# Fourier mixing and a maxout network on one core: earlier places for four planned steps, and the prologue's exponent matmuls held back by one group

## The chip, the cores and the metric

The kernel runs on one core of one Trainium2 chip. The metric is device microseconds of one execution. TensorE (PE) multiplies; VectorE (DVE), ScalarE (ACT) and GpSimd (POOL) work on tiles; SyncE (SP) only issues transfers, one after the other, and so do ACT and POOL for some of them. `PEld` is TensorE's weight load.

## The reference, cut to what matters

```python
X = np.fft.rfft(x, axis=1)                      # x: 8 x 3072 x 256, float32
Yr = Xr @ w_r - Xi @ w_i + b_r                  # w_r, w_i: 256 x 256
Yi = Xr @ w_i + Xi @ w_r + b_i
Yr, Yi = soft(Yr), soft(Yi)                     # sign(v) * max(|v| - 0.01, 0)
y = np.fft.irfft(Yr + 1j * Yi, n=3072, axis=1)
y = y.reshape(8 * 3072, 256)
h = np.maximum(np.maximum(y @ w1, y @ w2), y @ w3)   # 256 x 768 each
out = h @ w_out                                 # 768 x 256
```

## The kernel before

**The mathematics.** The transform of length 3072 = 96 x 32 is taken in two steps by matmuls. Stage `a` multiplies x (96 rows of 32 x 256) by a 96 x 96 table; its result goes through DRAM (`a_d`). Stage `b` reads it back in 12 groups of rows, k = 0 to 11 for each batch, and multiplies by the blocks of the second step (`mb`); stage `w` multiplies by w_r and w_i; the threshold follows; `finish_w` scales the result `u` to `vb`; stage `q` does the first step back and writes DRAM (`z_d`). `load_z` reads eight pieces of it for each batch, `split_z` splits each, and `inverse` does the last step and gives `y`. The network's three products are folded: h = w3 part + relu(y(w2 - w3) + relu(y(w1 - w2))), with the w3 part multiplied through w_out beforehand (`gh`, `gl`).

**The precision.** A value enters TensorE as two f16 halves: ACT makes the high one, DVE the low one, and a product takes three matmuls (`mm3`, L180 to L182). From batch 3 on x is first folded by its symmetry (`sum_x`), then split (`split_x`, tiles `xhl`), then multiplied (`stage_a`, L621).

**The order of the work.** After a prologue the network runs in 384 slots: 8 batches x 8 pieces x 6 blocks of 128 columns; a batch has `SLOTS` = 48. A slot does `up` for one block (tile `pu`, L1112 and L1120 its activations) and, three blocks late, `down` (tile `pd`). The Fourier work of later batches is laid between them: `events` holds (place, step) pairs, places counted in slots, and `run_until` runs those that are due three times in a slot, at its first third, its second and its end. While batch b-1 is in the network, stages b, w and q of batch b run, and stage a of batch b+1. During the last piece of batch b-1 the first piece of `z` of batch b is read and split, and the first `inverse` of batch b runs.

**The steps around the change.** For group k of a batch, `load_a` reads 256 KB of `a_d` into a buffer `ab` (SP, L681; one of the eight `raw` buffers, which x's second half `x2`, the moved `vb` and the weights use too); `split_a` makes the high half (ACT, L692), the low half (DVE, L695) and moves both within the core by four 64 KB transfers (SP, L700); `stage_b` multiplies (tile `px`, L790). `stage_q` of group 11 writes the last rows of `z_d` (ACT, L943; its transfers L947); `load_z` reads a piece of 384 KB (SP, L1012) into the one buffer `zq`; `split_z` makes the halves `zh` and `zl` (ACT L174, DVE L175) and moves them in eight transfers to `ze` (SP, L1062; four where the piece isn't the first of a batch); `inverse` multiplies (tile `pi`, L1077). In the prologue, groups k = 0 to 11 of batch 0 run in a loop, with the weights' loads (`load`), maxima (`largest`, L373), exponents (`exponent_of`) and splits (`phase`) laid out by `planned(k, ...)`.

`exponent_of` turns a tile's column maxima into one exponent: DVE reduces to a column (`col`, L270), TensorE spreads it (tile `pt`, L274), DVE finishes. All behind the column goes through `later`: in the slots it waits for a later third; in the prologue it is called at once:

```python
    def later(fn):
        if "slot" in st:
            waiting.append((st["slot"], fn))
        else:
            fn()
```

The framework gives each engine's instructions their final order. It takes what it reckons ready, earlier places in the program first; so a place is a rank, not a time. Instructions traced `in_turn` stay behind the slot's last activation, and `load_a` behind the last `load_z`.

Of the kernel before, what the change touches and what calls it, by code (L numbers as in the profile page):

```python
# [101 lines left out]
def fourier_maxout_kernel(  # L102
# [12 lines left out]
    NJP = 12  # L115
    SLOTS = NCH * NF
    NATIVE = 2 * NCH
    HALF_X = 3 * NCH
# [8 lines left out]
    st = {}  # L127
# [6 lines left out]
    def split_scaled(hi, lo, src, scale):  # L134
        h = hi if hi.dtype == F16 else hi.bitcast(F32)
        nc.scalar.activation(out=hi, in_=src, func=AF.Copy, scale=scale)
        return nc.vector.scalar_tensor_tensor(
            out=lo, in0=src, scalar=scale, in1=h, op0=ALU.mult, op1=ALU.subtract
        )
# [5 lines left out]
    def later(fn):  # L145
        if "slot" in st:
            waiting.append((st["slot"], fn))
        else:
            fn()

# [17 lines left out]
    def split_later(hi, lo, src, scale=None):  # L168
        h = hi if hi.dtype == F16 else hi.bitcast(F32)
        if scale is None:  # L170
            nc.scalar.activation(out=hi, in_=src, func=AF.Copy)  # L171
            later(lambda: nc.vector.tensor_tensor(out=lo, in0=src, in1=h, op=ALU.subtract))  # L172
        else:
            nc.scalar.activation(out=hi, in_=src, func=AF.Copy, scale=scale)  # L174
            later(lambda: low(nc.vector.scalar_tensor_tensor(  # L175
                out=lo, in0=src, scalar=scale, in1=h, op0=ALU.mult, op1=ALU.subtract
            )))
# [62 lines left out]
    def load_fft_weights():  # L240
        ws = raw_tile("wst").rearrange("p (k c) -> p k c", k=KD)
        for i, w in enumerate((w_r, w_i)):
            nc.sync.dma_start(
                out=ws[:, :, i * D:i * D + D], in_=w.rearrange("(k p) d -> p k d", p=P)
            )
        return [ws[:, kd] for kd in range(KD)]

    def load_tables():
        rows = [b.rearrange("(r o d) -> r o d", r=1, o=1) for b in (b_r, b_i)]
        for c in range(2):  # L250
            nc.sync.dma_start(out=bias[64 * c:64 * c + 64, 0:1], in_=rows[c].broadcast_to([64, 1, D]))
        nc.sync.dma_start(out=qf, in_=mq[:, 0:2])
        nc.sync.dma_start(out=id_sb, in_=ident)
        st["tiled"] = s_tile("tiled")[:, 0:P]
        nc.sync.dma_start(out=st["tiled"], in_=mq[:, 26])
# [7 lines left out]
    def small(name, dt=F32, bufs=1):  # L263
        return fft.tile([P, 1], dt, name=name, bufs=bufs)
# [33 lines left out]
    def limits(name, total, one):  # L298
        low, add = small("low" + name), small("add" + name)
        nc.vector.tensor_scalar(  # L300
            out=low, in0=total, scalar1=-1.0, scalar2=one + 1.0, op0=ALU.mult, op1=ALU.add
        )
        nc.vector.tensor_scalar(out=low, in0=low, scalar1=28.0, scalar2=254.0, op0=ALU.max, op1=ALU.min)
        nc.vector.tensor_scalar(out=add, in0=total, scalar1=1.0, scalar2=-one, op0=ALU.mult, op1=ALU.add)
        return low, add
# [3 lines left out]
    def scale_fft_weights(ws):  # L309
        mx = fft.tile([P, KD], F32, name="mxc", bufs=1)  # L310
        for kd, t in enumerate(ws):
            nc.vector.tensor_reduce(
                out=mx[:, kd:kd + 1], in_=t[:, 0:2 * D], axis=AX.X, op=ALU.max, apply_absolute_value=True
            )
        def scales(e):
            st["lim", "x"] = limits("x", e, 142.0)
            st["sc"] = power("sc", e, -1.0, 267.0, 1)

        exponent_of(mx, "c", 23, 0xFF, 28.0, scales)
# [34 lines left out]
    class Weights:  # L354
# [83 lines left out]
        for v in range(0, FF, HALF) for i in range(3) for kd in range(KD)  # L438
    ], less=True)
    w_dn = Weights("d", [  # L440
        (woh[:, f], wol[:, f], out_v2[f * P:(f + 1) * P],
         out_v2[f * P:(f + 2) * P].rearrange("(k p) w -> p k w", p=P) if f + 1 < NF else None,
         [t[:, f:f + 2] for t in (woh, wol)] if f + 1 < NF else None)
        for f in range(NF)
    ])
# [32 lines left out]
    def pump(new=True):  # L478
        for u in list(reversed(running)):
            phase(*u)  # L480
            if not made[u]:
                running.remove(u)
        if units and new:
            running.append(units.pop(0))
            phase(*running[-1])
# [5 lines left out]
    def at(pos, fn, i, k=None, n=None):  # L491
        if n is None or 0 <= k < n:
            events.append((pos, len(events), fn, i))
# [482 lines left out]
    for q in range(EARLY, NB * NCH):  # L976
        b, i = divmod(q, NCH)
        p = i if b == 1 else 9 + 5.2 * i if b == 2 else (b - 2) * SLOTS + 5.6 * i
        at(p - (3 if b == 1 else 5 if b == 2 else 8), load_x, q)
        if q >= HALF_X:  # L980
            at(p - 1, sum_x, q)
        at(p, split_x, q)
        at(p + 1, stage_a, q)
        if q >= HALF_X:
            p = 9 + 5 * i if b == 3 else (b - 3) * SLOTS + 5.5 * i + 5
            at(p - 4, load_m, q)
            at(p, largest_m, q)
            if i == NCH - 1:
                at(p + 1, scale_m, b)
    for b in range(1, NB):  # L990
        for k in range(-2, NJP + 1):
            p = 8 + 2.13 * (k + 2) if b == 1 else (b - 1) * SLOTS - (1.2 if b > 2 else 0.4) + 2.72 * (k + 2)
            for d, fn, i in (
                (0, load_a, k + 3), (-1.4, split_a, k + 1), (1.6, finish_w, k - 1), (1, stage_b, k + 1),
                (4, stage_q, k - 1), (2, stage_w, k), (2.4, stage_w2, k),
            ):
                at(p + d, fn, b * NJP + i, i, NJP)
            if k == -2:
                at(p, load_a, b * NJP)

    def run_until(pos):
        while events and events[0][0] <= pos:
# [165 lines left out]
    def load_first_blocks(i, n=6):  # L1168
        k = slice(i, i + n)
        nc.sync.dma_start(out=mb_f[:, k], in_=mq[:, 2 + i:2 + i + n])  # L1170
# [25 lines left out]
    def planned(k, fn, *args):  # L1196
        plan[k].append((fn, args))
# [11 lines left out]
    planned(3, w_dn.load, 0)  # L1209
    planned(4, lambda: w_dn.load(2, [fft.tile([P, 2, D], F32, name="ru", tag="u", bufs=2) for _ in range(2)]))  # L1210
    planned(6, w_dn.load, 4)
    for k, n in ((4, 0), (5, 2), (5, 3), (7, 4)):
        planned(k, w_dn.largest, n)
    planned(7, w_dn.scale)
    for k, n in ((5, 0), (7, 2)):
        planned(k, prepare, w_dn, n)
        planned(k + 3, phase, w_dn, n)

    for k in range(-3, NJP + 1):
        for fn, i in (  # L1220
            (load_a, k + 3), (stage_b, k + 1), (stage_w, k), (finish_w, k), (stage_q, k - 1),
        ):
            if 0 <= i < NJP:
                if fn == stage_q and i == NJP - 1:
                    total = small("total")
                    nc.vector.tensor_tensor(out=total, in0=w_up.e, in1=w_dn.e, op=ALU.add)
                    st["lim", "u"] = limits("u", total, 271.0)
                fn(i)
        with tc.issue_after(st["ld"].ins):
            if k == -3:  # L1230
                fft_weights = load_fft_weights()
                load_first_blocks(2, 4)
            if k == -2:
                load_tables()
            if k == 0:
                scale_fft_weights(fft_weights)
                split_scaled(*(t.rearrange("p a b -> p (a b)") for t in (qh, ql, qf)), Q_SCALE)
            if k == 0:
                split_scaled(ft[:, 0], ft[:, 1], st["tiled"][:, 64:P], F_SCALE)
                split_scaled(qt[:, 0], qt[:, 1], st["tiled"][:, 0:64], Q_SCALE)  # L1240
            if k in (-2, 1, 4):
                load_first_blocks(2 * k + 10)
            for fn, args in plan[k]:
                fn(*args)
            if k == 6:
                whole = ga_sb.rearrange("p i e n m -> p (i e n m)")
                nc.sync.dma_start(out=whole, in_=ga[:, 0:2 * N2 * N1])
                first = fft.tile([N1, NQ * D], F32, name="xm", bufs=1).bitcast(F16)[:, 0:2 * NT]
                nc.sync.dma_start(out=first, in_=ga[:, 2 * N2 * N1:])
                st["ga"] = first.rearrange("p (i n m) -> p i n m", i=2, n=NQ)  # L1250
            if 7 <= k < 12:
                load_x(NCH + k - 7)
            if k == 8:
                units += [(w_up, n) for n in (6, 8, 10)] + [(w_dn, n) for n in (3, 4)]
            if k in (8, 9, 10):
                pump()
# [130 lines left out]
```

## Time and profile before

| | |
|---|---|
| time, median of 3 runs | 1776.3 us (1773.79 to 1778.37) |
| the profiled execution | 1774.88 us, of which the span is 1772.8 us |
| PE busy | 98% of the span, 15747 matmuls |
| DVE, ACT, POOL busy | 68%, 66%, 16% |
| mean granted TensorE clock | 0.997 |
| transfers | `zq<-z_d` 384.0 KB, `ab<-a_d` 256.0 KB, `ab<-ab` 64.0 KB, median 4.5, 4.7 and 3.1 us to landing |

A row of the timeline gives the start, the length, the engine (`SPq` is a transfer being issued), the line, what is written and read, the shape, how many instructions are merged, and in brackets the engine's idle time before it and what ended that.

### The profile page before, as it was taken

The numbers are of one execution on the slowest core, as the hardware profiler recorded it, in microseconds if no ns is written. First come the engines' busy times: TensorE is split into PE (matmuls) and PEld (weight loads), VectorE is DVE, ScalarE is ACT, GpSimd is POOL, SyncE is SP. The second block draws the span as 40 slices with busy tenths as digits, with TensorE's granted clock in tenths as the row PEclk, the third lists the DMA queues.
The fourth block names the chain that finished last, engine by engine and source line by source line (L and its number), as shares of the span: only waits on it lengthen the run. The fifth ranks groups of instructions, "written<-read, shape, count | busy, mean of one in ns | idle before, by whom it ended". The sixth has DMA issues, their size and how long they took to land.

```text
span 1772.8 us, 40996 instructions
## 1 busy us (share of the span) xinstructions
PE 1732.1 (98%) x15747; PEld 1253.5 (71%) x15747; DVE 1211.4 (68%) x2525; ACT 1164.4 (66%) x2445; POOL 277.2 (16%) x505
## 2 busy tenths in 40 slices
PE   9999999999999999999999999999999999999999
PEld 4766777667776777767776677776777777777776
DVE  2887887577865788667875688766786467644332
ACT  4777676676765777666765677666776566655554
POOL 1001012112221112112221112211212100110000
PEclk9999999999999999999999999999999999999999
DMA  9766565467655577457765667555664444422111
GB/s 295 243 173 182 160 174 153 145 177 200 173 147 154 155 190 201 128 153 188 184 165 155 160 166 213 152 141 146 169 168 122 120 109 115 121 76 62 55 56 35
DMA packets 201936, 269.52 MB, mean 152 GB/s; under 512 B 30862, under 2 KB 149998, under 8 KB 201646
## 3 DMA queue, kind: packets, MB, share of 16 engines
q1 hardware_dynamic: 169502, 193.34, 42.3%
q0 software_dynamic: 24608, 66.62, 11.5%
q10 hardware_dynamic: 7632, 6.95, 1.4%
q8 instruction: 124, 2.03, 0.5%
q14 instruction: 70, 0.57, 0.1%
HBM read 124.31 MB, written 75.50 MB: 113 GB/s over the span
## 4 chain that ended last, share of the span: by engine, by line
PE 75%; DMA 8%; DVE 6%; issue 5%; ACT 4%; SPq 2%; POOL 0%; ACTq 0%; DVEq 0%; POOLq 0%
PE pu L180 11%; PE pu L182 11%; PE pu L181 11%; PE pd L180 8%; PE pd L182 8%; PE pd L181 8%; PE py L180 3%; PE py L182 3%; PE py L181 3%; PE pi L1077 3%; DMA ab<-ab 2%; PE px L790 2%; PE pz L958 2%; PE pa L621 2%; ACT zh L174 1%
## 5 line engine op out<-in xcount | busy, mean ns | idle before, releaser
L180 PE MATMUL pu<-yh,wuh 128*128 128x384 f16 x1536 | 501.9, 327 | 0.2 <-ACT pu L1112 0.2
L182 PE MATMUL pu<-yh,wul 128*128 128x384 f16 x1536 | 501.0, 326 | 0.0
L181 PE MATMUL pu<-yl,wuh 128*128 128x384 f16 x1536 | 501.0, 326 | 0.0
L172 DVE TENSOR_TENSOR hh<-h,hh 128x384 f16<-128x384 f32 x384 | 212.7, 554 | 187.3 <-ACT hh L171 186.9
L180 PE MATMUL pd<-woh,hh 128*128 128x256 f16 x1152 | 314.1, 273 | 1.1 <-ACT o L1157 1.0
L182 PE MATMUL pd<-woh,hh 128*128 128x256 f16 x1152 | 314.1, 273 | 0.0
L181 PE MATMUL pd<-wol,hh 128*128 128x256 f16 x1152 | 313.9, 273 | 0.0
L1112 ACT ACTIVATE pu<-pu 128x384 f32<-128x384 f32 x384 | 184.2, 480 | 185.1 <-PE pu L182 174.9
L171 ACT ACTIVATE hh<-h 128x384 f16<-128x384 f32 x384 | 199.9, 520 | 71.9 <-DVE h L1116 65.2
L182 PEld LDWEIGHTS <-wul 128*128 128x128 f16 x1536 | 150.3, 98 | 99.8 <-issue 0.7
L180 PEld LDWEIGHTS <-wuh 128*128 128x128 f16 x1536 | 150.2, 98 | 92.7 <-issue 21.7
L181 PEld LDWEIGHTS <-wuh 128*128 128x128 f16 x1536 | 150.3, 98 | 72.8 <-issue 1.7
L631 POOL DMA_DIRECT2D a_d<-aq x160 | 94.6, 595 | 608.3 <-ACT aq L628 605.9
L1159 POOL DMA_DIRECT2D out_dram<-o x189 | 104.4, 558 | 461.6 <-ACT o L1157 456.9
L1120 ACT ACTIVATE h<-pu 128x384 f32<-128x384 f32 x258 | 125.4, 486 | 67.5 <-PE pu L182 64.2
L180 PE MATMUL py<-wch,tt 128*128 128x256 f16 x504 | 137.4, 273 | 1.3 <-ACT zs L964 0.6
L180 PEld LDWEIGHTS <-hh 128*128 128x128 f16 x1152 | 112.6, 98 | 35.2 <-issue 10.5
L182 PE MATMUL py<-wch,tt 128*128 128x256 f16 x504 | 137.4, 273 | 0.0
L181 PE MATMUL py<-wcl,tt 128*128 128x256 f16 x504 | 137.3, 272 | 0.0
L175 DVE SCALAR_TENSOR_TENSOR zl<-zq,s0u,zh 96x1024 f16<-96x1024 f32 (+1 forms) x70 | 81.6, 1173 | 80.4 <-ACT zh L174 80.4
L1091 DVE SCALAR_TENSOR_TENSOR y<-pi,ye 128x192 f32<-128x192 f32 x252 | 109.6, 508 | 33.9 <-ACT ye L1085 33.6
L181 PEld LDWEIGHTS <-hh 128*128 128x128 f16 x1152 | 112.7, 98 | 26.4 <-issue 1.9
(261 smaller groups left out, 3116.5 us busy)
## 6 DMA issues: line engine op xcount, KB each, us to landing
zq<-z_d SPq DMA_DIRECT2D x63, 384.0 KB, 4.5
out_dram<-o POOLq DMA_DIRECT2D x189, 128.0 KB, 3.6
ab<-a_d SPq DMA_DIRECT2D x84, 256.0 KB, 4.7
ab<-ab SPq DMA_DIRECT2D x336, 64.0 KB, 3.1
vb<-vb SPq DMA_DIRECT2D x308, 64.0 KB, 3.0
z_d<-zs POOLq DMA_DIRECT2D x70, 256.0 KB, 3.8
xm<-in_x_dram SPq DMA_DIRECT2D x40, 384.0 KB, 4.0
a_d<-aq POOLq DMA_DIRECT2D x160, 96.0 KB, 3.4
```

The lines of the kernel that those rows point to most:

```text
L171: nc.scalar.activation(out=hi, in_=src, func=AF.Copy)
L172: later(lambda: nc.vector.tensor_tensor(out=lo, in0=src, in1=h, op=ALU.subtract))
L175: later(lambda: low(nc.vector.scalar_tensor_tensor(out=lo, in0=src, scalar=scale, in1=h, op0=ALU.mult, op1=ALU.subtract)))
L180: nc.tensor.matmul(o, lh, rh, start=start, stop=False, **kw)
L181: nc.tensor.matmul(o, lh, rl, start=False, stop=False, **kw)
L182: st["mm"] = nc.tensor.matmul(o, ll, rh, start=False, stop=stop, **kw)
L631: nc.gpsimd.dma_start(out=av[1 - r, :, :, n:n + 512], in_=o[64 * h:64 * h + 48])
L1077: st["mm"] = nc.tensor.matmul(pv[:, e, n2], st["z"][e][:, n2, h * P:(h + 1) * P], ga_sb[:, i, e, c * NQ + n2], start=i == 0, stop=i == 1,)
L1091: nc.vector.scalar_tensor_tensor(out=yv[:, e], in0=pv[:, 0], scalar=(1 - 2 * e) * Y_SCALE, in1=ev, op0=ALU.mult, op1=ALU.add,)
L1112: st["act"] = nc.scalar.activation(out=p, in_=p, func=AF.Relu)
L1120: st["act"] = nc.scalar.activation(out=h32, in_=p, func=AF.Relu, scale=H_SCALE)
L1159: q.dma_start(out=out_v[b, c, t], in_=o)
```

## The change

Five edits, in the order of the diff:

1. `later` gets a third way: where `st["held"]` is a list, the step is put on it. The prologue's loop empties the list after each group's five steps and, for k = 0 to 10, starts a new one ahead of that group's planned work. An exponent's matmul and all behind it so come after the next group's stages.
2. `split_x` of batches 3 to 7 stands 0.4 slots earlier.
3. `split_a` stands at -2.2 in place of -1.4 slots (batches 3 to 7), or -1.6 (batches 1 and 2).
4. `stage_q` of group 11 stands at 3 in place of 4 slots; `load_a` of group 0 stands 2.5 slots earlier (batches 3 to 7).
5. In the prologue, the last maximum of w_out and its exponent move from k = 7 to k = 8; the splits of two pieces of w_out come at k = 9 and 10 (before: 8 and 10).

```diff
     def later(fn):
         if "slot" in st:
             waiting.append((st["slot"], fn))
+        elif "held" in st:
+            st["held"].append(fn)
         else:
             fn()
...
-        at(p, split_x, q)
+        at(p - 0.4 * (q >= HALF_X), split_x, q)
...
             for d, fn, i in (
-                (0, load_a, k + 3), (-1.4, split_a, k + 1), (1.6, finish_w, k - 1), (1, stage_b, k + 1),
-                (4, stage_q, k - 1), (2, stage_w, k), (2.4, stage_w2, k),
+                (0, load_a, k + 3), (-2.2 if b > 2 else -1.6, split_a, k + 1), (1.6, finish_w, k - 1),
+                (1, stage_b, k + 1), (4 if k < NJP else 3, stage_q, k - 1), (2, stage_w, k), (2.4, stage_w2, k),
             ):
                 at(p + d, fn, b * NJP + i, i, NJP)
             if k == -2:
-                at(p, load_a, b * NJP)
+                at(p - (2.5 if b > 2 else 0), load_a, b * NJP)
...
-    for k, n in ((4, 0), (5, 2), (5, 3), (7, 4)):
+    for k, n in ((4, 0), (5, 2), (5, 3), (8, 4)):
         planned(k, w_dn.largest, n)
-    planned(7, w_dn.scale)
+    planned(8, w_dn.scale)
     for k, n in ((5, 0), (7, 2)):
         planned(k, prepare, w_dn, n)
-        planned(k + 3, phase, w_dn, n)
+        planned(9 + n // 2, phase, w_dn, n)
...
                 fn(i)
+        for fn in st.pop("held", ()):
+            fn()
+        if 0 <= k < NJP - 1:
+            st["held"] = []
```

Here p = (b - 1) * 48 - 1.2 + 2.72 * (k + 2) for batches 3 to 7, with k from -2 to 12.

## Rows read from the trace of the kernel before

**Rows 1.** The page, part 1: busy time, share, instructions.
```profile
PE 1732.1 (98%) x15747; PEld 1253.5 (71%) x15747; DVE 1211.4 (68%) x2525; ACT 1164.4 (66%) x2445; POOL 277.2 (16%) x505
```
**Rows 2.** Waits of PE: us in total, times, longest.
```profile
PE px L790 <- DMA ab<-ab: 13.3, 10, 3.4
PE pi L1077 <- DMA ze<-zl: 7.1, 10, 1.1
...
PE pa L621 <- DVE xhl L175: 2.2, 7, 0.3
...
PE pd L180 <- ACT o L1157: 1.0, 1, 1.0
```
**Rows 3.** Timeline of PE: two matmuls, one behind the other.
```profile
778.77 0.27 PE L182 MATMUL pd<-woh,hh 128*128 128x256 f16 x1
778.88 0.27 PE L180 MATMUL pd<-woh,hh 128*128 128x256 f16 x1
```
**Rows 4.** Timeline of DVE and PE in the prologue, 76 to 78 us.
```profile
76.37 0.69 DVE L373 TENSOR_REDUCE mwd<-rw 128x2 f32<-128x512 f32 x1 [3.35 <-DMA rw<-in_moe_w_out_dram]
...
77.79 0.49 PE L274 MATMUL pt<-id_sb,col 128*128 128x128 f32 x2 [3.01 <-DVE col L270]
```
**Rows 5.** Timeline of PE: stage b's waits, group 0 of batches 3 to 6, then group 11.
```profile
565.39 0.28 PE L790 MATMUL px<-mb_all,ab 128*128 128x64 f16 x4 [1.27 <-DMA ab<-ab]
566.52 0.51 PE L790 MATMUL px<-mb_all,ab 128*128 128x64 f16 x12 [0.86 <-DMA ab<-ab]
...
778.20 0.51 PE L790 MATMUL px<-mb_all,ab 128*128 128x64 f16 x12 [2.01 <-DMA ab<-ab]
...
991.97 0.51 PE L790 MATMUL px<-mb_all,ab 128*128 128x64 f16 x12 [1.79 <-DMA ab<-ab]
...
1204.47 0.51 PE L790 MATMUL px<-mb_all,ab 128*128 128x64 f16 x12 [3.39 <-DMA ab<-ab]
...
1543.21 0.94 PE L790 MATMUL px<-mb_all,ab 128*128 128x64 f16 x16 [1.13 <-DMA ab<-ab]
```
**Rows 6.** Timeline of ACT and SP ahead of the wait at 778.20.
```profile
765.84 1.14 ACT L174 ACTIVATE zh<-zq,s0u 96x1024 f16<-96x1024 f32 x1
...
769.29 0.62 ACT L692 ACTIVATE ab<-ab 128x512 f16<-128x512 f32 x1
...
771.33 0.58 SPq L1012 DMA_DIRECT2D zq<-z_d  x1
772.01 1.24 SPq L700 DMA_DIRECT2D ab<-ab  x2
```
**Rows 7.** The chain that ended last: start, length.
```profile
772.64 5.43 DMA ab<-ab
```
**Rows 8.** The page, part 6: issuer, count, size, median us to landing.
```profile
zq<-z_d SPq DMA_DIRECT2D x63, 384.0 KB, 4.5
...
ab<-a_d SPq DMA_DIRECT2D x84, 256.0 KB, 4.7
ab<-ab SPq DMA_DIRECT2D x336, 64.0 KB, 3.1
```
**Rows 9.** Stretches: busy time (instructions) of PE, PEld, DVE, ACT, POOL; clock; DMA.
```profile
567.78:571.19 3.41, 3.41 (x30) 2.31 (x28) 1.78 (x5) 0.80 (x3) 0.00 (x0) 0.50 0.92 241
...
779.41:782.82 3.41, 3.41 (x29) 2.26 (x28) 1.68 (x4) 0.85 (x3) 0.00 (x0) 0.50 0.73 241
...
1201.00:1204.40 3.40, 0.08 (x3) 0.00 (x0) 1.16 (x2) 1.18 (x3) 0.27 (x1) 1.00 1.00 265
```
**Rows 10.** Timeline of ACT at the first and the last change of batch.
```profile
321.31 0.47 ACT L1112 ACTIVATE pu<-pu 128x384 f32<-128x384 f32 x1 [0.68 <-PE pu L182]
...
325.06 1.33 ACT L174 ACTIVATE zh<-zq,s0u 96x512 f16<-96x512 f32 x2 [0.63 <-issue]
...
1587.90 0.47 ACT L1112 ACTIVATE pu<-pu 128x384 f32<-128x384 f32 x1 [0.84 <-PE pu L182]
1588.29 1.32 ACT L174 ACTIVATE zh<-zq,s0u 96x512 f16<-96x512 f32 x2
```

## The prediction, on record before the changed kernel ran

> **What bounds the kernel.** I read the page's busy shares first, and in them TensorE alone: it is busy for 98% of the span, the next engine for 68% [rows 1]. So a change pays here only where TensorE stands idle, or where its clock is halved; the same work done sooner on another engine pays nothing by itself. The list of TensorE's waits came second. The reader is to see that few reasons hold nearly all of it: stage b waits for the moved halves of `ab` (13.3 us), the inverse for those of z (7.1 us), stage a for the low half of x (2.2 us) [rows 2], and one exponent's matmul in the prologue for its column (3.0 us) [rows 4]. Third came the timeline of each wait, for what is late ahead of it. One correction holds for all of them: a matmul's record is 0.27 us long while the next one starts 0.11 us behind it [rows 3], so TensorE really loses about 0.16 us more at each wait than the row says.
>
> Fourth I read the granted clock by stretches. Behind the waits of batches 3 and 4 it stands at 0.50, the lower of its two levels (1.2 GHz), for 3.41 us, in each of two places [rows 9]. At half the rate each such stretch costs half its length, 1.7 us. The longest wait left the clock at 1.00 although TensorE was busy for 0.08 of 3.40 us [rows 9], so a wait doesn't always bring this on.
>
> **The change, part by part.** No matmul, activation or byte is added. Everything moves.
>
> *The prologue.* DVE stands for 3.35 us until a load of w_out has landed, reduces it at 76.37, and TensorE, whose queue has the exponent's matmul in the middle of a group's eight, stands for 3.01 us [rows 4]. With the reduction one group later and its matmul behind the following group's stages, TensorE has a whole group's products between them. Gain 3.0 + 0.16 = 3.2 us. The lower bound is nothing: DVE may still meet the load early and hold up a threshold behind it. What follows (the exponents' small steps, the splits of w_out) gets one group's time less and is needed only in the network. I take the upper end, because DVE's wait alone stopped nothing here; TensorE stopped at the matmul.
>
> *The first group of batches 3 to 6.* Five rows: 1.27 + 0.86 + 2.01 + 1.79 + 3.39 = 9.3 us [rows 5], with five tails of 0.16 10.1 us. What is late is seen at 778.20. ACT makes the high half at 769.29; SP issues the read of the next z piece at 771.33 and the second pair of moves only at 772.01 [rows 6]; the last of that pair takes 5.43 us from issue to landing [rows 7], against a median of 3.1 us for this transfer [rows 8]. After the change `split_a` is due one slot earlier (a slot is 4.6 us on average, the span over 384), directly behind the split of z at 765.84, whose 1.14 us end at 766.98 [rows 6]: 2.3 us earlier. At 2.3 us all waits but the last would be gone and that one would keep 1.1 us. But the moves would also be ready ahead of the read of z, which waits for the same `zl`, and the 2.3 us by which they now exceed the median would go too, together 4.6 us. I take the whole 10.1 us; the lower bound is 2.3 us less at the batch with 3.39 us and nothing where the read stays ahead and ACT is crowded, some 5 us. The earlier first `load_a` is what makes the split possible there: it must have landed a slot sooner. The two half-clock stretches stand right behind two of these waits; without them 3.4 us more. Their lower bound is nothing, as I can't tell what else lowers the clock.
>
> *Later groups.* Every split of these batches moves by 0.8 slots. At group 11 of batch 7 the wait is 1.13 us [rows 5], with its tail 1.3 us, and a slot covers it. The other waits of the 13.3 us are 2.9 us in four places (13.3 less 9.3 and 1.1), two of them in batches 1 and 2, where the split moves by only 0.2 slots. I take 1.0 us of them; bounds nothing and 2.9. Sum 2.3 us.
>
> *v's last group.* The last rows of z are written a slot sooner, so z's first piece is read sooner. But its split can't begin ahead of the slot's own activation. At the first change of batch that one starts at 321.31 and the split at 325.06, so 3.3 us can be won; at the last they are at 1587.90 and 1588.29, back to back, and nothing can [rows 10]. Taking at each of the seven changes the smaller of this room and of the wait there gives 4.6 us, of the 7.1; with the tails of the three that vanish 5.2 us. Bounds nothing and 7.1.
>
> *x split sooner.* Seven waits of 0.3 us, 2.2 us together [rows 2]; a third of a slot is over a microsecond and covers each. With tails 3.3 us; I take two thirds, 2.2, because this split now comes next to those of z and `ab` in a batch's first slot, which lengthens ACT's queue there. Bounds nothing and 3.3.
>
> *What the moves cost.* New neighbours make new small waits. Those that the list shows today where nothing was planned, like the 1.0 us of `pd` for `o` [rows 2], are what I go by: four of that length, 4 us. The bounds are nothing and the 8 us of the first rival.
>
> Sum: 3.2 + 10.1 + 3.4 + 2.3 + 5.2 + 2.2 - 4 = 22.4 us. The profiled execution has 1774.9 us, 1.5 below its median (its span 1772.8 and 2.1 around it, in which nothing changes); 22.4 off the median of 1776.3 gives 1754.
>
> **A rule weighed against this.** The pair of moves behind the 384 KB read took 5.43 us, the median is 3.1 [rows 7, 8]: what SP issued ahead was served first. The Trainium skill, "DMA: Bandwidth & Descriptors", section "Queues, rings and completion order", says that SP has one ring on each of the 16 DMA engines and that descriptors are consumed in ring order; the trace agrees, by these 2.3 us. The rule speaks for the moves that now pass the read of z, and against the first `load_a`, which may now stand in front of z's moves.
>
> **The rivals.** *The early read in front of z's moves.* The 256 KB of `load_a` are now due while z's eight moves go out, on which the inverse waits. 384 KB cost 2.3 us, so 256 KB cost 1.6 us; at five changes of batch (for batches 3 to 7) 8 us, in place of the 4 that I subtract: a gain of 18, and if the inverse's 5.2 us go with it 13: a time of 1758 to 1763, say 1761. For it: the inverse has no room today, all its waits end with these moves. Against: in the plan the last rows of `a_d` stand at 40.2 slots and the read at 44.3, so it may be through before z's moves begin. By the rule named above the price is the same, as order in the ring is all it tells.
>
> *The order stays.* A place is only a rank; if the framework keeps the read of z ahead of the second pair and the splits where they are, only the exponent's 3.2 us remain, with small gains: 1772. Against: the split stands one slot later than its neighbour z and follows the slot's activation, which a rank does change.
>
> *The early read blocks SP: slower.* If the framework puts the first `load_a` ahead of z's moves and its buffer or the last rows of `a_d` aren't there, SP stands and z's moves stand behind it; TensorE then waits at `pi`. It decides from 22.4 / 5 = 4.5 us at each of the five changes on; at 6 us the kernel takes 1784. For it: all of these steps share SP. Against: eight `raw` buffers, of which at that place I count at most five held (two `ab`, two `x2`, one `vb`).
>
> **The numbers.** Chances: forecast 0.60, the read in front 0.16, the order stays 0.15, SP blocked 0.09. A difference of 0.3%, 5.3 us, is about what a measurement of this kernel can tell from no change. Faster by more: the first two and a little of the third, 0.77; within: 0.14; slower: 0.09. The range reaches up to 1773, which leaves out the blocked queue and part of the third case, and down to 1745, where the upper ends of all terms would lie (3.2 + 10.1 + 3.4 + 4.4 + 7.1 + 3.3 = 31.5): together under 2 in 10.
>
> **What would show it.** Right: no wait of `pt` near 75 us; no wait of `px` at the first group of batches 3 to 6, ACT's `ab` within a microsecond behind `zh`, the moves of `ab` issued ahead of the read of z; the clock at 1.00 there; the waits of `pi` gone at three changes of batch and kept at the others. Wrong: `pi` waits above 7.1 us with `load_a` issued among z's moves (first rival); `px` waits as before with the read between the pairs (second); SP idle until `a_d` or a buffer (third). The prediction fails most likely at the 4 us for new waits, which no row of the kernel before can show.

## The result and the profile after

The changed kernel takes 1745.8 us (median of 4 runs, 1742.64 to 1747.86), the kernel before, run beside it, 1775.1 (4 runs, 1771.74 to 1778.37). The ratio is 0.983, 95% interval 0.981 to 0.986: 29 us faster. The forecast was 1754 with a range from 1745; the time lies at that range's lower edge. The profiled execution took 1742.64 us, of which 1740.8 are the span: 32.0 less than the span before. In the changed file the lines stand two further down (L790 is L792, L1077 is L1079, L692 is L694).

The page's busy shares, of the kernel after:

```profile
PE 1721.4 (99%) x15747; PEld 1249.0 (72%) x15747; DVE 1208.6 (69%) x2525; ACT 1161.8 (67%) x2445; POOL 277.9 (16%) x505
```

The same 15747 matmuls, and 10.7 us less busy time [rows 1]: part is clock, part is records that had been stretched by waits inside (the X edit, below). TensorE's waits in the kernel after (us in total, times, longest):

```profile
PE pi L1079 <- DMA ze<-zl: 2.6, 4, 0.9
PE px L792 <- DMA ab<-ab: 1.6, 2, 0.9
PE pz L773 <- DVE mxu L755: 1.5, 1, 1.5
...
PE pd L182 <- ACT o L1159: 0.8, 2, 0.4
```

`px` for `ab` falls from 13.3 to 1.6, `pi` from 7.1 to 2.6, `pa` for `xhl` L175 and `pt` for `col` have left the list [rows 2, 4]. One wait is new, 1.5 us of the prologue's `pz`. The timeline at the network's change from batch 2 to 3 and of the opening of batch 4 behind it, where the wait of 2.01 us had been [rows 5, 6] (ACT, then SP, then PE):

```profile
750.79 1.14 ACT L176 ACTIVATE zh<-zq,s0u 96x1024 f16<-96x1024 f32 x1
751.83 0.61 ACT L694 ACTIVATE ab<-ab 128x512 f16<-128x512 f32 x1
...
733.17 0.39 SPq L683 DMA_DIRECT2D ab<-a_d  x1
...
736.82 1.16 SPq L1064 DMA_DIRECT2D ze<-zh  x2
...
753.26 1.14 SPq L1064 DMA_DIRECT2D ze<-zl  x2
754.49 2.67 SPq L702 DMA_DIRECT2D ab<-ab  x4
757.22 0.58 SPq L1014 DMA_DIRECT2D zq<-z_d  x1
...
761.13 0.63 PE L792 MATMUL px<-mb_all,ab 128*128 128x64 f16 x16
```

`split_a` follows the split of z at once, all four moves are issued ahead of the next read of z, and `px` begins without a wait. Counted from z's split (765.84 before, 750.79 after), ACT makes the high half 2.4 us sooner. But SP is still issuing z's moves until 754.40, so the last of the four moves is issued only 1.0 us sooner [rows 6]. The rest is time to landing. The second pair of moves, in the kernel before and then after (from the issues: count, size, median us to landing):

```profile
ab<-ab SPq DMA_DIRECT2D x2, 64.0 KB, 5.4
```
```profile
ab<-ab SPq DMA_DIRECT2D x2, 64.0 KB, 2.1
```

The early 256 KB read goes out 3.65 us ahead of z's first moves, not among them; at the other four changes it is 3.2 to 4.3 us. At four of the five SP had first stood idle in front of it until the last rows of `a_d` had landed. SP's waits from 727 to 735 us (us in total, times, longest):

```profile
SPq L683 <- DMA a_d<-aq: 4.2, 2, 4.0
```

It held nothing up, because z's moves became due only behind the read. Stretches behind the former waits of batches 4 and 6 (busy time of PE, PEld, DVE, ACT, POOL; granted clock; DMA share; GB/s):

```profile
761.00:765.00 4.00, 4.00 (x58) 3.24 (x57) 2.53 (x5) 2.88 (x8) 0.83 (x2) 1.00 0.99 327
1174.00:1178.00 4.00, 4.00 (x59) 3.22 (x57) 2.14 (x4) 3.04 (x8) 1.67 (x3) 1.00 1.00 305
```

The clock stays at 1.00 (2.4 GHz), with the transfer engines at least as full as before [rows 9]. In the whole execution no stretch is at 0.50 but the very end; before there were three of 3.41 us, two behind `px` and one at 31.89 in the prologue.

Where the 32.0 us came from I read by slots: the start of the first `pu` of each of the 384 slots in both traces, and where the difference of the two steps.

| place | gain in the traces, us | term of the forecast, us |
|---|---|---|
| prologue, up to the first `pu` (111.83 to 107.93), its new waits included | 3.9, of it 1.7 the clock at 31.89, 1.1 more ahead of group 3, 1.1 behind it | 3.2 |
| openings of batches 3 to 6, in order 3.4, 3.2, 2.1, 3.8, and 1.2 in the two slots behind | 13.7 | 10.1 + 3.4 |
| later groups (0.6, 0.6, 1.6) | 2.8 | 2.3 |
| x split: 4 x 1.02, 1.82, 0.34 | 6.2, of it 2.2 also with a's edits alone | 2.2 |
| `pi` rows, 7.1 to 2.6 | 4.5 | 5.2 |
| new small waits, all else | about 1 gained | -4 |

### The profile page after: what moved, and what is told of

It is laid out like the page before. It is cut to its first block, busy times and chain, and to the rows that moved or that the text cites. A ratio compares the mean times of both kernels' runs of the same rounds, so it can differ in the third digit from the quotient of the medians.

```text
span 1740.8 us, 40997 instructions
## 1 busy us (share of the span) xinstructions
PE 1721.4 (99%) x15747; PEld 1249.0 (72%) x15747; DVE 1208.6 (69%) x2525; ACT 1161.8 (67%) x2445; POOL 277.9 (16%) x505
## 4 chain that ended last, share of the span: by engine, by line
PE 81%; issue 6%; DVE 4%; DMA 4%; ACT 3%; SPq 1%; POOL 0%; ACTq 0%; DVEq 0%; POOLq 0%
PE pu L182 12%; PE pu L184 12%; PE pu L183 12%; PE pd L182 8%; PE pd L183 8%; PE pd L184 8%; PE py L182 3%; PE py L184 3%; PE py L183 3%; PE pi L1079 3%; PE px L792 2%; PE pa L623 2%; PE pz L960 2%; PE pa L640 1%; DMA z_d<-zs 1%
```

## The experiments

Ratios are to the kernel before run beside each of them, with a 95% interval; gains are that ratio times the time before.

**One part at a time.** The four parts, each alone in the kernel before. The X edit:

```diff
-        at(p, split_x, q)
+        at(p - 0.4 * (q >= HALF_X), split_x, q)
```

> Of the change only x's split 0.4 slots earlier. By the prediction's term (seven waits of 0.3 us with tails of 0.16 us each) at most 3.3 us less, the seven waits of pa for xhl gone. By the rival, that a wait at these matmuls, four of which run side by side in the array, hides more than its record shows: 5 to 6.5 us less, about 1.0 us at the eighth slot of each of four batches, with the same rows gone.

Measured 1769.8 us, 0.999 (0.997 to 1.001): no change. The waits of `pa` are gone, but new waits of `px` have come. Of this run, a line of the list of waits; one of the new ones, from PE's timeline; a wait in the prologue, from PE's timeline; and the stretch around it, with the columns of the stretches above:

```profile
PE px L790 <- DMA ab<-ab: 14.5, 13, 2.8
```
```profile
1229.48 0.51 PE L790 MATMUL px<-mb_all,ab 128*128 128x64 f16 x12 [1.15 <-DMA ab<-ab]
```
```profile
74.40 2.05 PE L771 MATMUL pz<-uf,qf 128*128 128x512 f32 x2 [2.75 <-DVE mxu L760]
```
```profile
73.70:83.90 10.20, 7.03 (x19) 5.19 (x20) 5.06 (x23) 6.04 (x11) 0.00 (x0) 0.50 0.79 198
```

The total of 14.5 us says little, as three runs below whose network is that of before have 10.8 to 14.3. But three of these waits (0.50, 0.23 and 1.15 us) stand in the slot right behind one that the edit shortened, where no other run has one, and those slots are 0.66, 0.38 and 1.31 us longer: there the gained time is handed on to the next wait for a transfer. That it stays where those are gone, the times don't show (1749.8 us without X and 1748.8 with it, below). The stretch at half clock is chance: the prologue is the same as before here, yet it met a second wait. This run also shows what a wait at `pa` hides. The twelve small `pa` matmuls of one group in the kernel before, and then those of this run:

```profile
584.18 0.64 PE L621 MATMUL pa<-xhl,zeros 48*64 48x512 f16 x4
585.14 0.40 PE L621 MATMUL pa<-xhl,zeros 48*64 48x512 f16 x2 [0.32 <-DVE xhl L175]
...
585.81 0.62 PE L621 MATMUL pa<-xhl,zeros 48*64 48x512 f16 x6
586.36 0.28 PE L182 MATMUL py<-wch,tt 128*128 128x256 f16 x1
```
```profile
588.36 1.16 PE L621 MATMUL pa<-xhl,zeros 48*64 48x512 f16 x12
589.44 0.28 PE L180 MATMUL py<-wch,tt 128*128 128x256 f16 x1
```

Without the wait the twelve take 1.08 us to the next product; with it 2.18, of which two `py` in between are 0.2. So 0.9 us are lost where the row says 0.32: these matmuls run beside each other, their records overlap, and idle time counts only from the end of the last. The slot is 0.87 us shorter in this run at four places. The tail here is about 0.55 us, not the 0.16 of full-size matmuls.

The edits of a's split and first read:

```diff
-                (0, load_a, k + 3), (-1.4, split_a, k + 1), (1.6, finish_w, k - 1), (1, stage_b, k + 1),
+                (0, load_a, k + 3), (-2.2 if b > 2 else -1.6, split_a, k + 1), (1.6, finish_w, k - 1), (1, stage_b, k + 1),
...
-                at(p, load_a, b * NJP)
+                at(p - (2.5 if b > 2 else 0), load_a, b * NJP)
```

> Of the change only a's first read 2.5 slots and a's splits 0.8 (0.2) slots earlier. Forecast by the sum's terms: 10.1 + 3.4 + 2.3 = 15.8 us less, px waits gone at group 0 of batches 3 to 6, both half-clock stretches behind them gone. Rival: the read stands in front of z's moves, pi waits grow from 7.1 to about 15 us, and the gain is about 8 us. Second rival: without x's split moved too, ACT's first slots are crowded and half of the px waits stay: 7 us.

Measured 1759.3 us, 0.993 (0.990 to 0.995): 13.1 us. `px` for `ab` is at 1.9 us in 4 places, and the four openings gain 3.39, 3.18, 2.07 and 3.79 us, to 0.01 us as in the whole change, each against the one trace of before. `pi` stays (8.2 us).

The edit of v's last group:

```diff
-                (4, stage_q, k - 1), (2, stage_w, k), (2.4, stage_w2, k),
+                (4 if k < NJP else 3, stage_q, k - 1), (2, stage_w, k), (2.4, stage_w2, k),
```

> Of the change only v's last group multiplied a slot earlier. Forecast by the room between the slot's activation and z's split: 4.6 us of pi waits gone (batches 1, 2 and 4 in the main, 5.2 us with tails), those at the changes to batches 3, 5, 6 and 7 left within 0.4 us. Rival: all waits but those of the last two changes go, because they hang on other things than z's read: over 5.5 us. Third: the waits stay because the moves to ze are held by SP: under 1.5 us.

Measured 1766.0 us, 0.997 (0.995 to 0.999): 5.3 us. `pi` falls to 4.8 us (6.5 to 8.3 in the runs with v's place of before and SP's queue untouched), and no change of batch is without a wait: some 0.4 us is left at five of the seven, 1.0 and 1.7 at the others.

The prologue: `later` with its held list, and w_out's maximum, exponent and splits at k = 8, 9 and 10 (the rest of the diff).

> Of the change only the prologue (the held exponents and w_out's maximum a group later). Forecast: the 3.0 us wait of pt gone, first slot 3.2 us sooner, and nothing else: 3.2 us less. Rival: the new wait of pz for a threshold, 1.5 us near 94 us, belongs to the prologue's change and is paid back: 1.7 us less. If the first slot comes 3.9 us sooner or more, the clock's half stretch near 32 us has gone with it.

Measured 1769.3 us, 0.998 (0.997 to 1.000): 3.2 us. `pt` no longer waits; `pz` waits 1.5 and 0.9 us for `mxu` in its place. The four parts sum to 1.8 + 13.1 + 5.3 + 3.2 = 23.4 us, 2 to 6 less than the whole in its two measurements (25.4 and 29.4). Each of these numbers is uncertain by 3 to 6 us, so that the whole is more than its parts isn't shown.

**The whole, and the whole less one.** The changed kernel again; without the X edit; without the early `load_a`.

> The whole change once more, beside the four part runs: for adding up. First measured ratio 0.9834, so about 29 us less than the kernel before. If the parts of the first four runs (13.1, 5.3, 3.2 and 1.8 us by their ratios) simply add, 23.4 us; if x's part is worth more where a's split has moved too, 27 to 30 us.

> The change without x's earlier split. If the parts add, it is 1.8 us (the part alone) behind the whole change. Theory: alone, x's split was laid ahead of a's split on ACT and DVE in a batch's first slot and so lengthened the px waits (14.5 us there, 13.3 before), which hid what it gave; with a's split moved it gives 5 to 6 us, at slot 8 of four batches about 1.0 us each, so this kernel is 5 to 6 us behind the whole change, with seven or eight pa waits in its list and px waits as short as in the whole change.

> The change without the earlier read of a's first rows (their split still a slot sooner). Theory of the prediction: the read is what lets the split stand there; without it the split waits on ACT for the landing, about 1 us at batches 3 to 6, the px waits stay short since there are 3 us of room, and the time is within 2 us of the whole change. Rival: ACT stands in order behind the late read, the activations of pu with it, and half of the px waits come back: 5 to 8 us behind the whole change. Rival on the queue: the early read costs z's moves 1.6 us at five changes of batch, so without it the kernel is 3 to 8 us faster.

Measured 1748.8 us, 0.986 (0.982 to 0.989), for the whole; 1749.8, 0.987 (0.983 to 0.990), without X; 1750.4, 0.986 (0.983 to 0.990), without the early read. In time the three can't be told apart. The traces can. Without X the four slots lose 0.67 us each and two others 1.0 and 0.3, together 4.0; the rest of the 6.2 in the table stands in the trace of a's edits alone (4 x 0.35 and 0.8). `pi` waits again at three changes where the whole kernel has none (0.35, 0.57, 0.40 us; the slots lose 0.73, 0.52, 0.45). So a part of `pi`'s gain is the X edit's, though why isn't shown. Of these 5.7 us the medians show 1.0: in the same two traces other slots go the other way, the two largest by 1.2 and 1.0 us. Without the early read the four openings gain exactly what they gain with it (3.40, 3.18, 2.07, 3.79), with the split in the same place; about 0.35 us of `pi` comes back at three changes, and a wait of `pa` for ACT's `hh` opens elsewhere (1.6 us, with a stretch at half clock behind it).

**Is it the order in SP's queue, or the full engines?** The kernel before, in which ACT issues the second pair of group 0's moves:

```diff
-                    nc.sync.dma_start(
+                    (nc.scalar if i and k % NJP == 0 else nc.sync).dma_start(
                         out=both[64 * i:64 * i + 64, :, b], in_=parts[64 * b:64 * b + 64, i]
```

> The kernel before, with the two moves of a's low halves of group 0 issued by ACT in place of SP: in batches 3 to 6 nothing else in any engine's order differs, and the split stands as late as before. By the order of the queue (the moves are late because SP's 384 KB read of z stands ahead of them) they land about 2.3 us sooner, the px waits fall from about 11 to 14 us to 3 to 6, and the kernel is 5 to 9 us faster. By the rival, that the DMA engines are simply full there, the moves land as late as before and nothing changes beyond 2 us.

Measured 1767.1 us, 0.996 (0.994 to 0.998): 7.3 us, with the split as late as before. A line of the list of waits; from the timeline the same opening of batch 4 (ACT and SP) and the wait that stayed, of batch 3 (PE); and the pair at the opening of batch 4 among the issues:

```profile
PE px L790 <- DMA ab<-ab: 5.2, 6, 3.2
```
```profile
770.65 0.61 ACT L692 ACTIVATE ab<-ab 128x512 f16<-128x512 f32 x1
772.54 1.29 ACTq L700 DMA_DIRECT2D ab<-ab  x2
...
772.68 0.58 SPq L1012 DMA_DIRECT2D zq<-z_d  x1
...
567.85 0.51 PE L790 MATMUL px<-mb_all,ab 128*128 128x64 f16 x12 [3.19 <-DMA ab<-ab]
```
```profile
ab<-ab ACTq DMA_DIRECT2D x2, 64.0 KB, 4.3
```

The moves still go out beside the 384 KB read, but in another queue. The kernel stands 1.36 us later here than before [rows 6], so they are issued 0.83 us sooner; the wait that vanished was 2.01 us, and at batch 6 3.39 us became 0.23. From issue to landing they now take 4.3 us at batches 4 and 5, against 5.4 and 5.3 behind the read in SP's queue, and they still land 0.4 us behind the read. Ahead of the read, in the kernel after, it is 2.1. So of the 3.3 us between first and last in the queue, 1.0 to 1.1 are the order in SP's queue. The other 2.2 stay in another queue too: that fits the rival, that the engines are shared with the read, which no run separates from the smaller transfers around it. At batch 3 the remedy failed: ACT's issue of the pair took 2.33 us instead of 1.29, and the wait grew from 0.86 to 3.19. Why that one differs is open; SP's issue of the read took 1.58 us there in the kernel before, against 0.58 at the other openings, so the place may be slow for either queue.

**Which edit of the prologue does it?** The held exponents alone, and w_out's steps one group later alone.

> The kernel before with the held exponents alone; w_out's last maximum stays at k = 7, its splits at 8 and 10. Theory (either edit of the prologue is enough, because TensorE stopped only at the matmul in the middle of a group): the 3.0 us wait of pt near 75 us is gone, no other wait of TensorE over 1 us takes its place ahead of 100 us, the prologue's end comes 3 us sooner. Rival (both edits are needed): DVE still stands 3.35 us for the load of w_out in the same place, the thresholds behind it are late, and a wait of pz for mxu of 1.5 us or more appears between 73 and 90 us; the prologue's end comes at most 1.5 us sooner. Whole kernel: 0 to 4 us faster than before by the one, within 1.5 us of it by the other.

> The kernel before with w_out's last maximum and exponent at k = 8 and its splits at 9 and 10, exponents' matmuls not held back. Theory (either edit is enough): DVE no longer meets the load early (its wait of 3.35 us falls under 0.5 us), the wait of pt falls from 3.0 us to under 0.5 us. Rival (both are needed): the matmul in the middle of a group's eight still waits 1 us or more for its column. Whole kernel: 0 to 4 us faster by the one, at most 2 us by the other.

Measured 1769.4 us, 0.9985 (0.997 to 1.000), and 1771.2, 0.9996 (0.998 to 1.001): neither differs from before by more than the measurement tells. In both traces `pt` doesn't wait, though DVE still stands 1.42 and 2.15 us for the load, so the late plan doesn't take that away; `pz` waits 1.3 us in the one and 0.9 in the other. The length of the prologue says more, from the first `px` of group 3 to the first `pu` (43.35 to 111.83 in the kernel before: 68.5 us). It hangs on when the last piece of w_out has landed, seen at DVE's reduction behind it (76.37, 33.0 us behind that `px`, in the kernel before):

| prologue | load landed, us behind the first `px` of group 3 | length, us |
|---|---|---|
| of before (v's last group alone, before, moves on ACT, a's edits alone, X alone) | 32.2, 33.0, 34.2, 35.7, 36.8 | 67.7, 68.5, 69.6, 73.7, 74.3 |
| with both edits (six traces) | 34.5 to 35.5 | 67.2 to 68.1 |
| held alone; late plan alone | 35.2; 33.1 | 67.5; 67.0 |

The later the load, the longer the prologue of before: `pt` waited 1.4 to 3.6 us, and in the three longest `pz` waited 1.6 to 2.8 us as well; in the two longest the clock was halved at these waits. With both edits a load as late as 35 us costs no more, 3.2 us less on average (70.8 less 67.6); in the profiled pair alone it was 68.5 to 67.3. The held exponents alone do the same at 35.2. For the late plan alone this isn't shown, as its load came early.

**The first rival by force.** The changed kernel, with the 256 KB read issued behind the first two of z's eight moves at the five changes:

```diff
-                at(p - (2.5 if b > 2 else 0), load_a, b * NJP)
+                b > 2 or at(p, load_a, b * NJP)
...
+                    if pieces == 2 and 1 < b < NB - 1 and not (i or cols.start):
+                        with tc.issue_after(st["zm"].ins): load_a((b + 1) * NJP)
```

The other six moves are held behind that read in the same way.

> The changed kernel with one thing forced: at the changes of batch from 2 to 3 on, the 256 KB read of group 0 is issued behind the first two of z's eight moves and ahead of the other six, where the first rival of the prediction saw it. If the order in SP's queue is what a transfer waits for (384 KB in front cost 2.3 us), the last of z's moves land 1.6 us later plus 0.4 us of issue at each of five changes: pi waits grow from about 3 us to 10 us or more, the time is 8 to 10 us above the changed kernel's. If transfers only share the engines, or TensorE has other work there, pi stays under 5 us and the time within 2 us. If the read now comes too late for split_a, px waits of 1 us and more come back at group 0 of batches 3 to 6 as well.

Measured 1752.3 us, 0.988 (0.986 to 0.990), by the ratios 5 to 9 us above the changed kernel's two measurements. A line of the list of waits, and the timeline of SP and PE at the network's change from batch 2 to 3:

```profile
PE pi L1081 <- DMA ze<-zl: 7.6, 8, 1.5
```
```profile
742.56 1.15 SPq L1065 DMA_DIRECT2D ze<-zh  x2
743.99 0.39 SPq L683 DMA_DIRECT2D ab<-a_d  x1
744.44 1.15 SPq L1065 DMA_DIRECT2D ze<-zl  x2
...
749.48 0.37 PE L1081 MATMUL pi<-ga_sb,ze 96*128 96x48 f16 x8 [1.26 <-DMA ze<-zl]
```

The rival's mechanism exists: `pi` goes from 2.6 to 7.6 us, and the five changes give 0.74, 1.26, 1.13, 1.01 and 0.65 us. But that is 1.0 us a change, between what the two theories expected; 0.6 of it is the issue alone (z's moves go out over 5.6 us in place of 5.0). The 1.6 us that the prediction scaled by bytes from the 384 KB read's 2.3 us were too many.

**The two leftover waits.** The changed kernel, with the last group's threshold behind the previous group's on DVE, and ACT issuing the second pair of batch 1's group 0:

```diff
-        nc.vector.tensor_tensor_reduce(
+        with tc.issue_after(st["thr"].ins) if last else nullcontext(): nc.vector.tensor_tensor_reduce(
...
-                    nc.sync.dma_start(
+                    (nc.scalar if i and k == NJP else nc.sync).dma_start(
```

> The changed kernel with its two leftover waits treated: in the prologue the last group's threshold begins behind the previous group's on DVE (the wait of pz for mxu, 1.5 us at 93.75, should go), and the second half of the moves of batch 1's group 0 is issued by ACT in place of SP (the px wait of 0.9 us at 160.25 should go). Theory (what is left is these single waits): both waits are gone, span 2 to 3 us under the changed kernel's. Rival (the sum of waits is no longer what sets the time; others open elsewhere as in the X edit alone): one or both go but as much idle time turns up at other places, time within 1 us of the changed kernel's.

Measured 1745.5 us, 0.985 (0.983 to 0.987), against 0.983 (0.981 to 0.986) and 0.986 (0.982 to 0.989) for the changed kernel: the same. Both waits are gone and the prologue is 0.9 us shorter, but `pi` stands at 4.1 us instead of 2.6 (3.2 in the changed kernel's second trace) and the wait of 0.3 us for `zh` is 0.9. The time can't tell 2 us from nothing; the trace speaks for the rival, that the waits that are left are traded and not removed.

## Why the prediction was right, and which terms were mis-sized

The mechanism and the direction were right. The sum was 7 us short of the 29 in the medians of the first measurement (10 in the profiled pair) and 3 short of the 25 in the second, whose interval, 19 to 31 us, holds it.

*The openings of batches 3 to 6* were right in what moves and in the sum, 13.5 us forecast with the clock and 13.7 found, but the sum owes something to luck. The forecast had the moves landed 4.6 us sooner, 2.3 by the earlier split and 2.3 by passing the read; at batch 4 it was some 4.3, of which 1.0 is earlier issue and 3.3 the passing. Nor is the 5.43 us all order in SP's queue: the moves on ACT win back 1.1 of what the forecast put at 2.3. And the profiled run of before had long waits there: in six traces with these openings as before they cost 7.9 to 14.8 us more than in the kernel after, 11.5 on average. One sentence failed: that the early `load_a` makes the split possible. Without it the openings gain the same.

*The clock* was right on average over the whole execution. The mean granted clock of the 29, 17 and 23 runs of the kernel before loses 4.5, 5.9 and 4.3 us a run ((1 - clock) x time), that of the changed kernel 1.3 and 1.5: 3.0 to 4.4 us against the forecast 3.4. Where the stretches fall changes from run to run: at these four openings it was none in two of the six traces and 10.2 us in another.

*The prologue* was right in size as a mean, 3.2 us, and wrong in detail: in the profiled pair only 1.1 of the 3.9 is there, because waits of 1.5 and 0.4 us for `mxu` took the place of the 3.0. The other 2.8 lie ahead of group 3, where the other traces with and without the edits don't differ (but for a half-clock stretch in some of either kind), so I take them for chance. The forecast counted on both edits; holding the exponents back was enough.

*Later groups*: 2.8 us found against 2.3; in the second trace of the whole, a wait of 1.0 us at one of these places is back.

*v's last group*: 4.5 us found against 4.6 of waits, and waits gone at three changes, but the agreement is luck. The room on ACT and the waits gave the changes to batches 1, 2 and 4; those to 3, 4 and 5 are the ones without a wait, and without the X edit or with v's edit alone no change is. The edit alone takes away 2.2 us. The room that I counted decides less than I thought. At the first change, in the kernel after:

```profile
316.53 0.47 ACT L1114 ACTIVATE pu<-pu 128x384 f32<-128x384 f32 x1 [0.84 <-PE pu L184]
316.92 1.33 ACT L176 ACTIVATE zh<-zq,s0u 96x512 f16<-96x512 f32 x2
```

The split moved the full 3.4 us, from 3.75 us behind the activation [rows 10] to 0.39, yet its 1.66 us of waits only fell to 0.47: I take the eight moves' issue and landing to be what is left. At the three middle changes this rest is gone only with the X edit.

*The x split* was mis-sized in the traces: 2.2 us forecast, 4.0 in the slots of the two that differ by X alone (the table's 6.2 holds 2.2 of a's edits). The row of 0.32 us hides 0.9, and I gave it the tail of a full-size matmul. In time, 1.8 us alone and 1.0 in the whole are neither told from nothing nor from the 2.2.

*The 4 us for new waits* was the step that failed most, as the prediction had said of it. The new ones are 1.5 and 0.4 us of `pz`, while old accidental ones went (`pd` for `o` from 1.0 to 0.8, `pa` for L172 from 0.8 to 0.4): near nothing in the sum. One new cost is steady: a slot at the start of batches 3 to 6 is 0.28 us longer in every trace with a's edits, 1.1 us together. With `px`, `pa` and `pi` late no more, TensorE has, I take it, fewer places where a shift turns into a wait.

*The rivals.* The first has its price measured at 5 us of waits instead of 8, and did not take place: the read is issued ahead of the moves. The second did not either, as SP's rows show. The third came closer than its 0.09 says: its sign, SP idle until `a_d`, was there at four of five changes for 4.1 to 4.5 us. SP was idle in front of the read with 3.2 us or more to spare, and so no move of z stood behind it.

*The working* has three small slips: 4.6 and three tails of 0.16 are 5.1 and not 5.2, the upper end of the later groups is 4.2 by its own bounds and not 4.4, and 2.3 x 256/384 is 1.5 and not 1.6. None matters to the forecast.

The Trainium skill, "DMA: Bandwidth & Descriptors", section "Queues, rings and completion order", says that SP and ACT each own one ring on every one of the same 16 DMA engines, and that an engine consumes descriptors in ring order. The runs agree at batches 4 and 5 by the 1.0 to 1.1 us that the pair wins on ACT; the 2.2 us by which it stays slower there than ahead of the read are no matter of order in one ring. At batch 3 (0.86 us to 3.19) the runs don't agree, and for z's moves, where more than half of the 1.0 us is the issue, order alone gives no price.

## What to carry to other kernels

A wait behind a transfer can be the transfer's place in its issuer's queue, or what moves beside it. Here 64 KB took 5.4 us to land behind a 384 KB read, 4.3 beside it from another engine's queue, and 2.1 ahead of it. So look at what the queue issued just ahead, and first make the producer a little sooner so that the order flips; the other queue gave a third of that, and made one place of four worse. When one engine is at 98%, a wait removed just ahead of another wait can be handed on to it: look for new waits right behind. Before pricing a wait by its row, see whether the matmuls there run side by side: the row can show a third of the loss.

## What the runs showed that I had not expected

The times of one kernel scatter: the kernel before ranges from 1764 to 1787 us (69 runs on three chips, standard deviation 3.5 to 5.1 us on each), the changed one from 1743 to 1751 (10 runs, 1.4 and 2.2). Part of it is the clock: stretches at half clock, most of 3.41 us, two of 6.8 and one of 10.2, come at waits of some 1 to 3 us, at other places in each run, and are fewer where the waits are gone. Another part is the prologue: a load that landed up to 4.6 us later in one execution than in another moved its end by up to 6.5 us (67.7 to 74.3), the half clock included. So the waits of one profiled run, from which the forecast was added up, can be off by several us from those of the next.
